# Attention and SwiGLU on one core: a gap inside two weight arrays, and the identity matrix from GpSimd's count

## The chip, the cores and the metric

The kernel runs on one core of a Trainium2 chip. The metric is the device time of one execution in microseconds (us), the median of several runs. Five engines work side by side, each through its own queue in order: TensorE (PE in the profile; PEld are its weight loads), VectorE (DVE), ScalarE (ACT), GpSimd (POOL) and SyncE (SP), which here issues DMAs. They wait for each other by semaphores.

## The reference

Block-causal attention over 8 batches, 8 heads, 576 positions and a head size of 64, and behind it a gated feed-forward (SwiGLU) over all 4608 tokens, all in fp32:

```python
scores = scale * np.matmul(q, k.transpose(0, 1, 3, 2))
scores = np.where(mask, scores, -1000000000.0)      # mask: block of the query >= block of the key, blocks of 64
attn = np.exp(scores - np.max(scores, axis=-1, keepdims=True))
attn = attn / (np.sum(attn, axis=-1, keepdims=True) + 1e-09)
x = np.matmul(attn, v)                              # then [batch, seq, heads * 64]: 4608 tokens x 512
g = x @ w_gate                                      # 512 x 1536
out = (g * (1.0 / (1.0 + np.exp(-g))) * (x @ w_val)) @ w_out
```

q and k are drawn about four times larger than v. The weights arrive as 64-bit floats, which the kernel reads as pairs of 32-bit words and turns into fp32 itself.

## The kernel before

**Products in three.** TensorE multiplies in a rounded fp32 format. Each fp32 matrix is therefore held as a high part and a low remainder, and each product is taken as three: high by high, high by low, low by high (L1100 to L1102 for the products with w_gate and w_val, L1191 to L1193 for those with w_out). In the names a final 0 is the high part and 1 the low one: xhl0_0 and xhl0_1, g_even0 and g_even1.

**Tiles.** The feed-forward goes over 18 tiles of 256 tokens. For each it takes the 1536 columns of w_gate and w_val in twelve chunks of 128, two chunks a step, so six steps a tile and 108 in all. A step is 12 products with the even gate chunk, 12 with the odd one and 24 with w_val's two chunks (4 chunks of the contraction of 512, by 3 products, each 128 x 256 columns), and 12 products with w_out (128 x 512). The weights are the stationary operand of the first 48, x is the moving one; for w_out the hidden values (hhl) are stationary.

**Where the weights lie.** w_gate and w_val stay in SBUF: `g_odd` and `g_even` hold the odd and the even chunks of w_gate, `v_all` all of w_val, each as a high and a low array of [128, 4, columns]. They are allocated in this order: ident, ones and two single columns, g_odd, v_all, a gap of 64 bytes, g_even, and then the pools (v, ob, parts, xhl, wo, hhl, t and so on). Their lengths are such that g_odd and v_all start 64 bytes past a multiple of 128, and g_even and everything behind it at a multiple of 128. `w_at` gives one chunk of 128 columns. Six chunks of w_out are parked, until they are stored, in places of w_gate and w_val that are not yet filled (`AWAY`); the others pass through the pool wo.

**The start.** TensorE turns q and k by products with `ident`, the 128 x 128 identity. VectorE makes it: it fills a row of `t` with 0, 1, 2, ... by doubling (L308 to L311), transposes 32 of them to get each partition's own number (L312), adds 32, 64 and 96 for the other quarters (L315), and compares (L316). GpSimd meanwhile fills v, ob and part of parts with zeros (L260, L281, L234). GpSimd's later work is the maximum over partitions (`partition_all_reduce`, L709).

**The order of the work.** The kernel writes down some thousands of tasks with an engine, an estimated cost and a rank, and `in_order` plays them through once at build time: it takes for each free engine the ready task of lowest rank, and what comes out is the program, with each engine's queue in that order. The change alters neither costs nor ranks nor the number of tasks. What stands before the tasks (the constants, the identity, the first zeros) is issued first.

Of the kernel before, what the change touches and what calls it, by code (L numbers as in the profile page):

```python
# [18 lines left out]
def kernel(  # L19
# [21 lines left out]
    P = 128  # L41
# [156 lines left out]
    g_odd = [const.tile(half_w, F32R, name=f"g_odd{x}") for x in range(2)]  # L198
    v_all = [const.tile(whole_w, F32R, name=f"v_all{x}") for x in range(2)]
    const.tile([P, 16], F32, name="gap")  # L200
    g_even = [const.tile(half_w, F32R, name=f"g_even{x}") for x in range(2)]

    def w_at(which, x, i):

        if which:
            return v_all[x][:, :, i * P : (i + 1) * P]
        return (g_odd if i % 2 else g_even)[x][:, :, i // 2 * P : (i // 2 + 1) * P]

# [86 lines left out]
    pool_of(psum, "gv", 2, [([P, 2 * XT], F32)])  # L297
    pool_of(psum, "po", 1, [([P, 2, DM], F32)])

    first_of = [("v", ""), ("ob", "signs" if wide else "out"), ("parts", "pair"), ("xhl", ""), ("wo", "raw"), ("hhl", "")]  # L300
    for tag, variant in first_of:
        for place in range(len(slots[tag])):
            tiles_of(tag, place, variant)


    scratch = tiles_of("t", 0)[0]
    count, mine = scratch[:, 0:P], scratch[:, P : P + 32]
    nc.vector.memset(count[:, 0:1], 0.0)  # L308
    for i in range(7):
        n = 2**i  # L310
        nc.vector.tensor_scalar(count[:, n : 2 * n], count[:, 0:n], float(n), None, ALU.add)  # L311
    nc.vector.transpose(mine, count[:, 0:32])  # L312
    for i in range(1, P // 32):
        rows = slice(32 * i, 32 * (i + 1))
        nc.vector.tensor_scalar(mine[rows, 0:1], mine[rows, 0:1], 32.0 * i, None, ALU.add)  # L315
    nc.vector.tensor_scalar(ident, count, mine[:, 0:1], None, ALU.is_equal)  # L316

    x_d = dram.tile([DM, NT], F32, name="x_d")
    s_d = dram.tile([H, NT], F32, name="s_d")
# [594 lines left out]
    def weight(i, kind):  # L914
# [11 lines left out]
        wo = Buf("wo", "out") if kind == 2 and not away else None  # L926
        fs = slice(i * P, (i + 1) * P)

        parts = 1 if wo else NDC

        def part(j):
            if wo:
                return wo[0][:, j : j + 1]
            which, c = away or (kind, i)
            return w_at(which, j, c)

# [11 lines left out]

        def words_of(j):
            w = raw[0].rearrange("p (n t) -> p n t", t=1 + wide)[:, :, j]  # L950
            return w.rearrange("p (n m) -> p n m", n=parts)

        y = Buf("ob", "signs") if wide else None


        def signs():
            w = words_of(1).bitcast(F32)
            to = y[0].rearrange("p (n m) t -> p n m t", n=parts)[:, :, :, 1]
            nc.scalar.mul(to, w, 2.0**-60)  # L959

        def scaled():
# [2 lines left out]


        def fraction():
            s = y[0].rearrange("p m t -> p (m t)").bitcast(I32).rearrange("p (n m) -> p n m", n=parts)
            nc.vector.scalar_tensor_tensor(
                words_of(0), words_of(0), 29, s, ALU.logical_shift_right, ALU.bitwise_or
            )  # L970
# [21 lines left out]
        if kind == 2:  # L992
            w_kept[i] = t, wo, part

            def store():
                if wo:
                    nc.sync.dma_start(out=wo_d[i], in_=wo[0].bitcast(F32))
                    return
                for j in range(2):
                    nc.sync.dma_start(  # L1000
                        out=wo_d[i][:, j].rearrange("p (n m) -> p n m", n=parts), in_=part(j).bitcast(F32)
                    )

            t = dma(R, 5e5, store, [t], [wo] if wo else [], 2 if away else 1, packet=512 if away else 4096)
            if away:
                before_place.append((t, away))
# [59 lines left out]
    def feed_forward(j, t0, w, xs):  # L1066
# [19 lines left out]
        def up(i, which, prev):  # L1086
# [3 lines left out]
            for y in range(2):  # L1090

                for ds in [range(NDC)] if j >= FINE else [[d] for d in range(NDC)]:

                    def products(ds=ds, y=y):
                        hi, lo = (w_at(which, k, i + y) for k in range(2))
                        o = ps[0][:, y * w : (y + 1) * w]
                        for d in ds:
                            xhi, xlo = (xs[d][1][k] for k in range(2))
                            first, last = d == 0, d == NDC - 1
                            nc.tensor.matmul(o, lhsT=hi[:, d], rhs=xhi[:, 0:w], start=first, stop=False)  # L1100
                            nc.tensor.matmul(o, lhsT=hi[:, d], rhs=xlo[:, 0:w], start=False, stop=False)  # L1101
                            nc.tensor.matmul(o, lhsT=lo[:, d], rhs=xhi[:, 0:w], start=False, stop=last)  # L1102

                    ts = add(
                        "PE",
                        mm_us(w, w, w) * len(ds),
                        rank(i),
                        products,
                        [ts, *(xs[d][0] for d in ds), w_done[i + y, which]],
                        [ps, *(xs[d][1] for d in ds)],  # L1110
                    )
                    ts.prev = prev
                    prev = ts if j >= FINE else None
# [3 lines left out]
        for i in range(0, NFC, 2):  # L1117
# [41 lines left out]
            for y in range(2):  # L1159
# [3 lines left out]
                else:  # L1163
# [5 lines left out]
                    chain["wo"] = wl  # L1169

                    def w_part(k, wo=wo):
                        return wo[0][:, k : k + 1]

                took.append((wl, wo, w_part, away))

# [7 lines left out]
            for piece in pieces:  # L1183

                def products(i=i, piece=piece, hh=hh, took=took):
                    for y, m in piece:
                        whi, wlo = (took[y][2](k) for k in range(2))
                        bs = slice(y * w + m * P, y * w + (m + 1) * P)
                        po = sums(m).rearrange("p (n m) -> p n m", n=whi.shape[1])
                        hi, lo = hh[0][:, bs], hh[1][:, bs]  # L1190
                        nc.tensor.matmul(po, lhsT=hi, rhs=whi, start=i + y == 0, stop=False)  # L1191
                        nc.tensor.matmul(po, lhsT=hi, rhs=wlo, start=False, stop=False)  # L1192
# [221 lines left out]
```

## Time and profile before

| | |
|---|---|
| median of 3 runs | 1178.03 us (1176.53 to 1178.63) |
| the profiled execution, own time | 1175.4 us |
| its span, first to last instruction | 1173.6 us |
| TensorE busy | 1145.5 us (98%), 8512 matmuls |
| TensorE weight loads | 1024.7 us (87%) |
| VectorE, ScalarE busy | 758.9 us (65%), 620.4 us (53%) |
| GpSimd busy | 325.5 us (28%) |
| mean granted TensorE clock | 0.996 of full speed |
| DMA | 197.40 MB, 168 GB/s mean |

The profile is of one execution and has its own time; comparisons with other kernels go by the medians of runs. A matmul's duration in it is from its start to the modelled end of its pipeline, longer than the distance between two starts: how fast TensorE goes is read from the distances. A share of busy time is a mean over stages; here the first 75 us differ from the rest.

### The profile page before, as it was taken

The numbers are of one execution on the slowest core, as the hardware profiler recorded it, in microseconds if no ns is written. First come the engines' busy times: TensorE is split into PE (matmuls) and PEld (weight loads), VectorE is DVE, ScalarE is ACT, GpSimd is POOL, SyncE is SP. The second block draws the span as 40 slices with busy tenths as digits, with TensorE's granted clock in tenths as the row PEclk, the third lists the DMA queues.
The fourth block names the chain that finished last, engine by engine and source line by source line (L and its number), as shares of the span: only waits on it lengthen the run. The fifth ranks groups of instructions, "written<-read, shape, count | busy, mean of one in ns | idle before, by whom it ended". The sixth has DMA issues, their size and how long they took to land.

```text
span 1173.6 us, 21780 instructions
## 1 busy us (share of the span) xinstructions
PE 1145.5 (98%) x8512; PEld 1024.7 (87%) x8512; DVE 758.9 (65%) x1230; ACT 620.4 (53%) x1114; POOL 325.5 (28%) x139
## 2 busy tenths in 40 slices
PE   5889999999999999999999999999999999999998
PEld 4568778898898989988998899898989899999997
DVE  6988988575887668768575859575767533323222
ACT  6978876546573837465656555555646312212111
POOL 3222100144535251434444334252432500000000
PEclk9989999999999999999999999999999999999999
DMA  8658756766564756656565565655663445444432
GB/s 225 188 151 219 201 187 226 206 178 166 169 148 137 198 164 167 195 166 168 152 188 160 152 177 163 187 146 161 164 202 108 145 148 197 140 167 136 143 134 100
DMA packets 266982, 197.40 MB, mean 168 GB/s; under 512 B 195264, under 2 KB 231376, under 8 KB 266880
## 3 DMA queue, kind: packets, MB, share of 16 engines
q1 hardware_dynamic: 264304, 195.29, 56.9%
q8 instruction: 67, 1.10, 0.4%
q10 hardware_dynamic: 2576, 0.72, 0.3%
q14 instruction: 35, 0.29, 0.1%
HBM read 171.57 MB, written 24.38 MB: 167 GB/s over the span
## 4 chain that ended last, share of the span: by engine, by line
PE 85%; DVE 5%; ACT 4%; DMA 3%; issue 1%; POOL 1%; SPq 1%; ACTq 0%; DVEq 0%; POOLq 0%
PE gv L1100 16%; PE gv L1102 15%; PE gv L1101 15%; PE po L1191 7%; PE po L1193 7%; PE po L1192 7%; PE at L777 7%; PE at L564 6%; DVE sc L733 1%; DVE mx L705 1%; DMA wo<-in_moe_w_val_dram 1%; POOL mx L709 1%; DMA wo<-in_moe_w_out_dram 1%; ACT ob L959 1%; PE at L648 1%
## 5 line engine op out<-in xcount | busy, mean ns | idle before, releaser
L709 POOL PARTITION_ALL_REDUCE mx<-mx x80 | 144.1, 1850 | 408.7 <-issue 135.2
L1100 PE MATMUL gv<-xhl,v_all 128*128 128x256 f32 x864 | 241.8, 280 | 0.8 <-DVE t L1136 0.7
L1102 PE MATMUL gv<-xhl,v_all 128*128 128x256 f32 x864 | 239.7, 277 | 0.0
L1101 PE MATMUL gv<-xhl,v_all 128*128 128x256 f32 x864 | 239.3, 277 | 0.0
L828 POOL PARTITION_ALL_REDUCE mx<-mx x48 | 178.9, 3775 | 201.4 <-DVE mx L705 192.8
L1136 DVE SCALAR_TENSOR_TENSOR t<-t,gv 128x512 f32<-128x512 f32 x108 | 74.0, 685 | 215.4 <-ACT t L1133 215.2
L1100 PEld LDWEIGHTS gv<-xhl,v_all 128*128 128x128 f32 x864 | 162.1, 188 | 4.9 <-issue 2.5
L1101 PEld LDWEIGHTS gv<-xhl,v_all 128*128 128x128 f32 x864 | 162.3, 188 | 0.6
L1102 PEld LDWEIGHTS gv<-xhl,v_all 128*128 128x128 f32 x864 | 162.2, 188 | 0.2
L1133 ACT ACTIVATE t<-gv 128x512 f32<-128x512 f32 x108 | 64.6, 598 | 171.2 <-PE gv L1102 171.1
L1191 PE MATMUL po<-wo,hhl 128*128 128x512 f32 x372 | 147.7, 397 | 0.0
L1192 PE MATMUL po<-wo,hhl 128*128 128x512 f32 x372 | 145.6, 391 | 0.0
L1193 PE MATMUL po<-wo,hhl 128*128 128x512 f32 x372 | 145.1, 390 | 0.2 <-DVE hhl L1149 0.2
L1146 ACT CAST hhl<-t 128x512 fp32r<-128x512 f32 x108 | 67.0, 620 | 132.1 <-DVE t L1141 129.7
L733 DVE TENSOR_TENSOR sc<-sc,mx 128x640 f32<-128x640 f32 (+6 forms) x168 | 122.7, 765 | 11.7 <-POOL mx L709 11.6
L737 ACT ACTIVATE sc<-sc 128x1024 f32<-128x1024 f32 (+3 forms) x104 | 106.0, 1029 | 45.3 <-DVE sc L733 44.9
L1100 PE MATMUL gv<-xhl,g_even 128*128 128x256 f32 x432 | 123.7, 286 | 0.0
L1102 PE MATMUL gv<-xhl,g_even 128*128 128x256 f32 x432 | 122.2, 283 | 0.4 <-DVE g_even L981 0.4
L1101 PE MATMUL gv<-xhl,g_even 128*128 128x256 f32 x432 | 122.1, 283 | 0.0
L1100 PE MATMUL gv<-xhl,g_odd 128*128 128x256 f32 x432 | 120.7, 279 | 0.0
L1101 PE MATMUL gv<-xhl,g_odd 128*128 128x256 f32 x432 | 119.6, 277 | 0.0
L1102 PE MATMUL gv<-xhl,g_odd 128*128 128x256 f32 x432 | 119.6, 277 | 0.0
(171 smaller groups left out, 2368.8 us busy)
## 6 DMA issues: line engine op xcount, KB each, us to landing
wo<-wo_d SPq DMA_DIRECT2D x200, 512.0 KB
out_dram<-ob SPq DMA_DIRECT2D x35, 256.0 KB
v<-in_v_dram SPq DMA_DIRECT2D x64, 128.0 KB
xt<-x_d SPq DMA_DIRECT2D x64, 128.0 KB
rt<-r_d SPq DMA_DIRECT2D x128, 64.0 KB
qk<-in_q_dram SPq DMA_DIRECT2D x112, 72.0 KB
qk<-in_k_dram SPq DMA_DIRECT2D x104, 72.0 KB
x_d<-xu SPq DMA_DIRECT2D x24, 288.0 KB
```

The costliest lines, as they stand in the source:

```text
L709: nc.gpsimd.partition_all_reduce(m, m, channels=P, reduce_op=bass_isa.ReduceOp.max)
L733: nc.vector.tensor_tensor(piece(c), scores_of(c), m, ALU.subtract)
L737: nc.scalar.activation(x, x, AF.Exp)
L777: nc.tensor.matmul(ps[0][own(x), 1 - i if sums else i, q0 - s0 : s1 - s0], lhsT=ones if sums else vt[0][:, 2 * lane + c, own(x)], rhs=sc[0 ...
L828: nc.gpsimd.partition_all_reduce(m, m, channels=P, reduce_op=bass_isa.ReduceOp.add)
L1100: nc.tensor.matmul(o, lhsT=hi[:, d], rhs=xhi[:, 0:w], start=first, stop=False)
L1101: nc.tensor.matmul(o, lhsT=hi[:, d], rhs=xlo[:, 0:w], start=False, stop=False)
L1102: nc.tensor.matmul(o, lhsT=lo[:, d], rhs=xhi[:, 0:w], start=False, stop=last)
L1136: nc.vector.scalar_tensor_tensor(t[0][:, 0:n], t[0][:, 0:n], 1.0, pg[0][:, 0:n], ALU.add, ALU.mult)
L1191: nc.tensor.matmul(po, lhsT=hi, rhs=whi, start=i + y == 0, stop=False)
L1192: nc.tensor.matmul(po, lhsT=hi, rhs=wlo, start=False, stop=False)
L1193: nc.tensor.matmul(po, lhsT=lo, rhs=whi, start=False, stop=i + y == NFC - 1)
```

## The change

Each g_even array becomes two halves of two contraction chunks each, with 16 words (64 bytes) between them; the 64-byte gap ahead of the arrays stays. All views of a chunk get one more dimension (half, chunk, column), for every array, so that one expression serves all; the products take `hi[:, d // 2, d % 2]` in place of `hi[:, d]`. Chunks of w_out that are parked in g_even are stored half by half.

The identity is made by GpSimd's `iota`, which writes column minus partition into `t`, and one VectorE comparison with zero. Its place is now ahead of the first zeros. With that `t` is allocated before v, and with the longer g_even arrays (12416 bytes for 12288) v, ob, parts, xhl, wo and hhl move by 2304 bytes and the pools behind them by 256.

```diff
+    rows_w = NDC * DFF // 4
+    g_even = [const.tile([P, 2, rows_w + 16], F32R, name=f"g_even{x}") for x in range(2)]
...
+        if w is None:
+            w = g_even[x][:, :, 0:rows_w].rearrange("p h (n f) -> p h n f", n=NDC // 2)
+        else:
+            w = w.rearrange("p (h n) f -> p h n f", h=2)
+        return w[:, :, :, i // 2 * P : (i // 2 + 1) * P]
...
+    scratch = tiles_of("t", 0)[0].bitcast(I32)[:, 0:P]
+    nc.gpsimd.iota(scratch, [[1, P]], channel_multiplier=-1)
+    nc.vector.tensor_scalar(ident, scratch, 0, None, ALU.is_equal)
...
-    scratch = tiles_of("t", 0)[0]
-    count, mine = scratch[:, 0:P], scratch[:, P : P + 32]
-    nc.vector.memset(count[:, 0:1], 0.0)
-    for i in range(7):
-        n = 2**i
-        nc.vector.tensor_scalar(count[:, n : 2 * n], count[:, 0:n], float(n), None, ALU.add)
-    nc.vector.transpose(mine, count[:, 0:32])
-    for i in range(1, P // 32):
-        rows = slice(32 * i, 32 * (i + 1))
-        nc.vector.tensor_scalar(mine[rows, 0:1], mine[rows, 0:1], 32.0 * i, None, ALU.add)
-    nc.vector.tensor_scalar(ident, count, mine[:, 0:1], None, ALU.is_equal)
...
+                halves = [slice(0, 2)] if away[0] or away[1] % 2 else [slice(x, x + 1) for x in range(2)]
                 for j in range(2):
-                    nc.sync.dma_start(
-                        out=wo_d[i][:, j].rearrange("p (n m) -> p n m", n=parts), in_=part(j).bitcast(F32)
-                    )
+                    for x in halves:
+                        nc.sync.dma_start(
+                            out=wo_d[i][:, j].rearrange("p (h n m) -> p h n m", h=2, n=parts[1])[:, x],
+                            in_=part(j)[:, x].bitcast(F32),
+                        )
...
-                            nc.tensor.matmul(o, lhsT=hi[:, d], rhs=xhi[:, 0:w], start=first, stop=False)
+                            nc.tensor.matmul(o, lhsT=hi[:, d // 2, d % 2], rhs=xhi[:, 0:w], start=first, stop=False)
```

GpSimd's queue at the start of the program, before. A row "ISA" without operands ahead of other work loads a code library of GpSimd; here it is library 1, which has the reduction over partitions (the rows "ISA" with mx).

```order
L260 MEMSET v_0_78 128x640
L260 MEMSET v_0_80 128x640
L281 MEMSET ob_0_82 128x512
L281 MEMSET ob_0_84 128x512
L234 MEMSET parts_1_87 128x64
L234 MEMSET parts_1_90 128x64
L709 ISA
L709 ISA mx_0_181<-mx_0_181 128x256 [waits DVE_49]
```

The same place after:

```order
L311 ISA
L311 IOTA t_0_78 128x128
L269 MEMSET v_0_81 128x640
L269 MEMSET v_0_83 128x640
L290 MEMSET ob_0_85 128x512
L290 MEMSET ob_0_87 128x512
L243 MEMSET parts_1_90 128x64
L243 MEMSET parts_1_93 128x64
L710 ISA
L710 ISA mx_0_170<-mx_0_170 128x256 [waits DVE_49]
```

Ahead of the zeros stand two new rows, a library load (L311; it is library 0, which has the count) and the count. The load ahead of the reductions is there in both.

VectorE's queue at the start, before, from its last constant to the first maximum:

```order
L192 MEMSET seen 128x1
L308 MEMSET t_0_117 128x1
L311 TENSOR_SCALAR t_0_117<-t_0_117 128x1
L311 TENSOR_SCALAR t_0_117<-t_0_117 128x2
L311 TENSOR_SCALAR t_0_117<-t_0_117 128x4
L311 TENSOR_SCALAR t_0_117<-t_0_117 128x8
L311 TENSOR_SCALAR t_0_117<-t_0_117 128x16
L311 TENSOR_SCALAR t_0_117<-t_0_117 128x32
L312 STREAM_TRANSPOSE t_0_117<-t_0_117 128x32
L311 TENSOR_SCALAR t_0_117<-t_0_117 128x64
L315 TENSOR_SCALAR t_0_117<-t_0_117 32x1 x3
L316 TENSOR_SCALAR ident<-t_0_117 128x128
```

And after:

```order
L190 MEMSET unseen 64x1
L192 MEMSET seen 128x1
L312 TENSOR_SCALAR ident<-t_0_78 128x128
L703 COPY mx_0_170<-at_0_160 128x2x128
L706 TENSOR_TENSOR mx_0_170<-mx_0_170,at_0_160 128x2x128
```

Twelve instructions are gone; the comparison is left, and now waits for GpSimd. On TensorE, ScalarE and the rest of VectorE and GpSimd the order is the same, and SyncE has four more stores.

## Rows read from the trace of the kernel before

**Rows 1.** Busy time by stretch (instructions); clock, DMA share and GB/s at the end.

```profile
0.00:75.00 75.00, 54.29 (x417) 37.74 (x418) 59.43 (x132) 56.79 (x112) 22.44 (x26) 0.95 0.72 189
75.00:1150.00 1075.00, 1071.39 (x7965) 969.07 (x7964) 694.87 (x1092) 560.24 (x998) 303.03 (x113) 1.00 0.57 169
```

**Rows 2.** TensorE's waits after 75 us: who for whom, us, times, longest.

```profile
PE at L777 <- ACT sc L469: 2.0, 2, 1.1
...
PE at L1191 <- DMA wo<-wo_d: 0.2, 1, 0.2
```

**Rows 3.** Timeline of TensorE in one late step: start us, duration, line, operands.

```profile
1109.11 0.28 PE L1100 MATMUL gv<-xhl,g_even 128*128 128x256 f32 x1
1109.22 0.28 PE L1101 MATMUL gv<-xhl,g_even 128*128 128x256 f32 x1
1109.34 0.28 PE L1102 MATMUL gv<-xhl,g_even 128*128 128x256 f32 x1
...
1110.54 0.28 PE L1100 MATMUL gv<-xhl,g_odd 128*128 128x256 f32 x1
...
1111.90 0.28 PE L1100 MATMUL gv<-xhl,v_all 128*128 128x256 f32 x1
```

**Rows 4.** TensorE's busy time with g_even alone, by stretch (number of products).

```profile
200.00:400.00 200.00, 30.23 (x216) 1.00 0.63 175
400.00:1173.60 773.60, 126.17 (x948) 1.00 0.53 158
```

**Rows 5.** The same with g_odd alone.

```profile
400.00:1173.60 773.60, 121.06 (x948) 1.00 0.53 158
```

**Rows 6.** Timeline of all engines at the start; in brackets the idle time before.

```profile
0.73 1.20 POOL L260 MEMSET v<- 128x640 f32 x2 [0.29 <-POOLq L1397]
...
1.69 0.97 SPq L754 DMA_DIRECT2D v<-in_v_dram  x2
...
2.85 0.23 POOL L234 MEMSET parts<- 128x64 f32 x2
2.98 3.77 SPq L387 DMA_DIRECT2D qk<-in_q_dram  x6
...
4.44 1.22 PE L411 MATMUL gv<-ident,qk 96*128 96x96 f32 x6 [4.44 <-DVE ident L316]
...
8.74 0.42 DVE L702 COPY mx<-at 128x256 f32<-128x256 f32 x1 [4.36 <-ACT mx L482]
...
8.78 2.44 PE L411 MATMUL gv<-ident,qk 96*128 96x96 f32 x12 [0.97 <-DMA qk<-in_q_dram]
9.09 0.41 DVE L705 TENSOR_TENSOR mx<-mx,at 128x256 f32<-128x256 f32 x1
...
9.59 2.11 POOL L709 PARTITION_ALL_REDUCE mx<-mx  x2 [6.51 <-DVE mx L705]
...
11.73 1.02 DVE L733 TENSOR_TENSOR sc<-at,mx 128x512 f32<-128x512 f32 x2 [2.24 <-POOL mx L709]
...
12.67 0.68 DVE L968 SCALAR_TENSOR_TENSOR wo<-wo,ob 128x512 int32<-128x512 int32 x1
...
13.90 0.69 DVE L973 SCALAR_TENSOR_TENSOR wo<-wo 128x512 int32<-128x512 int32 x1 [0.55 <-ACT wo L963]
...
15.75 4.20 POOL L709 PARTITION_ALL_REDUCE mx<-mx  x4 [4.05 <-DVE mx L705]
```

**Rows 7.** GpSimd's instructions of line 709 up to 12 us: count, duration ns, first and last start.

```profile
L709 POOLq MODIFY_POOL_CONFIG  x2: 7/7/7, 3.1 to 3.1; - x2
```

**Rows 8.** Waits of SyncE's queue in the first 30 us.

```profile
SPq L387 <- DMA qk<-in_k_dram: 0.8, 1, 0.8
```

**Rows 9.** The chain that ended last, 50 to 76 us: start, us, what.

```profile
55.77 4.29 PE po L777 x40
...
67.03 7.20 PE at L777 x40
```

## The prediction before the run

> **What bounds the kernel now.** I read the busy times by stretch first. From 75 us to 1150 us TensorE is busy 1071.39 of 1075.00 us; in the first 75 us only 54.29 us [rows 1]. So the program has two parts with different limits: a start-up in which TensorE waits for others, and a long part in which it alone sets the time. In the long part it waits for a DMA once, for 0.2 us, and five times in all for 3.4 us, the longest 2.0 us [rows 2]. A nanosecond off a matmul there comes off the time, and a microsecond lost at the start is not won back, as there are only 3.4 us of idle time to lose it in.
>
> Then the matmuls in order of time. In a step of the feed-forward the twelve products with an even gate chunk start at 1109.11, 1109.22, 1109.34 and so on; the first with the odd chunk starts at 1110.54 and the first with v_all at 1111.90 [rows 3]. Twelve even ones take 1.43 us, twelve odd ones 1.36 us, though shape, buffers of x and instructions are the same. The first even spacing is 0.11 us like those of the odd ones, the eleven others 0.12. The same difference over the whole stretch: from 400 us on 948 products with g_even hold TensorE 126.17 us and as many with g_odd 121.06 us [rows 4, 5].
>
> What differs is where the arrays lie. By the kernel's sizes g_odd and v_all start 64 bytes past a multiple of 128, g_even and all that is allocated after it, x's halves (xhl) among them, at multiples of 128. So with g_even the weights that are loaded for the next product and the columns that stream for this one have equal addresses modulo 128; with g_odd and v_all they are 64 apart.
>
> Last the start, in order of time. GpSimd's memset of v starts at 0.73; SyncE's queue puts the first loads of v at 1.69 and behind them six loads of q from 2.98 on; TensorE starts at 4.44, released by `ident`, and again at 8.78, released by a load of q; GpSimd's first reduction starts at 9.59 and the next four at 15.75, each released by VectorE's maximum [rows 6]. Between the last memset and the first reduction lie 6.51 us of idle time, and in their first moment, at 3.1 us, two records called MODIFY_POOL_CONFIG [rows 6, 7]: they belong to the row without operands that stands before the reductions in GpSimd's order, which loads the code library (number 1) that has the reduction.
>
> **The change part by part.** *The gap.* With 64 bytes between the two halves of each g_even array, the contraction chunks 0 and 1 stay at equal places, and 2 and 3 become like g_odd's: six products of twelve. Of the eleven long spacings six go, of 0.07/11 = 0.0064 us each, so 0.04 us a step. From 200 us on there are (216 + 948)/12 = 97 steps [rows 4]: 3.8 us. Before 200 us I count nothing: TensorE's spacings there are mixed, and up to 75 us it is not the limit. Bounds: nothing (if the place is not the cause), and 97 x 0.074 = 7.2 us if all eleven go because the new distances (x now lies 256 bytes on, modulo 512, against g_odd, v_all and half of g_even) matter beyond 128 bytes. I take 3.8, since odd and even rows differ in nothing else that I find.
>
> The Trainium skill speaks against this edit: "SBUF — State Buffer", "Who interferes with whom", gives TensorE two independent read ports, one for the moving operand and one for the weights, and says that TensorE never waits on anyone. By that rule the gap gives 0 and not 3.8 us; the 0.07 us between two groups of equal products [rows 3] disagree with it, but show no cause by themselves.
>
> *The identity.* Twelve small VectorE instructions go. That gives nothing: VectorE idles 4.36 us until 8.74 right behind them [rows 6]. In their place GpSimd counts, and the order has one more row without operands ahead of the count: a load of library 0. After the memsets library 1 has to be loaded again, as before. The length of a load stands nowhere in the trace. From below it is nothing (library 0 might be there already). From above the nearest row is the idle time of 6.51 us, into which the load of library 1 fits without delaying the reduction: that starts 0.09 us after its releaser, as the next one does. I take 6.2 us for either load, near that row, since the reduction is the only row by which a load shows at all; the first one may well be longer, because nothing bounds it.
>
> The Trainium skill ("GPSIMD Engine Reference", "2.1 Instruction dispatch") has about 6 us, 5.95 measured, for the first call to a freshly loaded kernel, without an instruction in the profile. By it the start would lose 5.5 us, and the sum would be +1.7; no run here shows it yet.
>
> What waits for that load? Everything on GpSimd's queue behind it, which before started at 0.73: the count (about 0.3 us, between a 64-column memset, two in 0.23, and a 640-column one, two in 1.20 [rows 6]), the memsets of v, and so the third entry of SyncE's queue, the load of v, which waits for them. So SyncE stands still for 6.2 + 0.3 = 6.5 us with all later inputs behind it: the rest of q, and the first weights. One thing is won back: SyncE's wait of 0.8 us for loads of k [rows 8], which ScalarE's queue issues and which will long be there. The transposes that began at 8.78, released by a load of q, come 6.5 - 0.8 = 5.7 us later. `ident` itself is ready at about 0.73 + 6.2 + 0.3 + 0.4 = 7.6, so TensorE starts at 7.7 and not 4.44: 3.3 late, hidden by the 5.7.
>
> The second load starts when the memsets end: 0.73 + 6.2 + 0.3 + 2.35 = 9.6 (before: from 0.73 to 3.08 [rows 6]). The first reduction then starts at 15.8, not 9.59, and ends 2.1 later, at 17.9. Behind it VectorE has 1.02 + 0.68 + 0.69 + 0.42 + 0.41 = 3.2 us of queue [rows 6] up to the maximum of the next reductions: 21.2 against 15.75, 5.5 late. That is just inside the 5.7. From there every wait of TensorE up to 75 us is ended by ScalarE or VectorE, which are as late, so the 5.7 us go through to the end.
>
> *The rest at nothing.* Four more stores are issued (the two even parked pieces, each half in two): 4 x 0.49 us on SyncE's queue [rows 6], covered as TensorE waits 0.2 us for a DMA after 75 us; at most 2.0 without that cover. Casts into g_even write the same elements through one more dimension. All other addresses move by multiples of 256 bytes, so they keep their place modulo 128.
>
> **The sum** against the profiled execution, 1175.4 us (span 1173.6 and 1.8 around it): +5.7 - 3.8 = +1.9 us. That run lies 2.6 us under the median of the runs shown, 1178.03. On the median: 1179.9 us.
>
> **The rivals.** *The loads are longer, and the second decides* (slower). Price of the second path: its lateness is T0 + T1 - 6.9 us (5.5 at 6.2 each), of the first T0 - 0.5; the second is the later one from T1 = 6.4 on. With 8 us each the start loses 9.1 us: +9.1 - 3.8 = +5.3, 1183.3 us. For it: the first load has no bound, and the second now runs beside weight loads that ran later before. Against it: the load of before fitted into 6.51 us beside loads of its own.
>
> *The library is at hand, or its load costs next to nothing* (faster). Then the start stays where it is, as GpSimd's memsets and count end before 4 us: -3.8, 1174.2 us. For it: the two records take 7 ns each [rows 7]. Against it: the program ends with library 1 in place, and runs again and again.
>
> *The place is not the cause*, by the skill's rule on the ports: the even products would be slow as the first of a step. Then 1178.03 + 5.7 = 1183.7 us. Against it: the first even spacing is a short one and the eleven behind are equal.
>
> *The distances matter beyond 128 bytes* and all long spacings go: 5.7 - 7.2 = -1.5, 1176.5 us.
>
> One thing can move any of these: near 67 us TensorE's granted clock lies at the lower of its two levels, 1.2 GHz (0.95 over the first 75 us [rows 1]; forty products take 7.20 us there and 4.29 us ten us earlier [rows 9]). With a later start that may fall elsewhere or not at all, up to 2.9 us to the better, and as much to the worse if it comes twice.
>
> **How the numbers follow.** A measurement of this kernel tells a difference from 0.2%, 2.4 us. My case, 0.44: mostly within 2.4 us, 1177.5 to 1182. Longer loads 0.23, place not the cause 0.10: slower. Load for nothing 0.15: faster. Larger distances 0.08: about no change. So faster 0.18, same 0.41, slower 0.41. The range of 8 in 10 goes from the case without a load, 1174.2, to loads of 8 us with a little more, 1185.5.
>
> **What would show it.** The first transpose near 7.7 us, the second near 14.5, the first reduction near 15.8 with an idle stretch before it that no engine ends, the count near 7 us; in late steps twelve even products in 1.39 us and odd and v_all ones unchanged at 1.36 and 2.72. Wrong: a count near 1 us (no load), twelve even products in 1.43 or 1.36, or a v_all spacing that has changed.

## The result and the profile after

The changed kernel takes 1181.31 us (median of 20 runs, 1179.26 to 1185.14), the kernel before 1176.84 (20 runs, 1174.90 to 1179.15). The ratio is 1.0037 with an interval of 1.0029 to 1.0045: 4.4 us slower, 3.4 to 5.3. Forecast were 1.9 us slower and a range of 1174.2 to 1185.5. That holds the result, and slower was one of the two likeliest outcomes; the likeliest case's own size was too small.

The profiled execution has a time of 1185.14 us and a span of 1183.4, the slowest of its 20. So the spans of the two profiles, 9.8 us apart, are not the effect of the change. A part of it is TensorE's clock in the first 75 us: its mean is 0.89 of full speed and not 0.95 [rows 1].

```profile
0.00:75.00 75.00, 51.23 (x363) 36.09 (x363) 50.89 (x106) 51.81 (x99) 20.15 (x25) 0.89 0.65 169
75.00:1150.00 1075.00, 1069.26 (x7951) 964.04 (x7952) 701.68 (x1102) 564.39 (x1007) 304.23 (x115) 1.00 0.58 169
```

The chain of waits shows the clock by three groups of forty equal products (start, us, what). One takes 4.29 us as before, at 2.4 GHz; two take 6.55 and 6.01, partly at 1.2 GHz, where the kernel before had one slow group [rows 9]. In this execution the granted clock is at 1.2 GHz in three stretches, 23.1 to 33.3, 50.4 to 57.2 and 77.7 to 81.1 us; in the profile before it is so from 66.1 to 72.9 and in the last 2 us.

```profile
52.64 6.55 PE po L778 x40
...
66.02 4.29 PE po L778 x40
...
77.28 6.01 PE at L778 x40
```

The start, in order of time, all engines (answers to [rows 6]):

```profile
7.96 0.23 POOL L311 IOTA t<- 128x128 int32 x1 [7.52 <-issue]
8.16 1.19 POOL L269 MEMSET v<- 128x640 f32 x2
8.23 2.31 DVE L312 TENSOR_SCALAR ident<-t 128x128 f32<-128x128 int32 x1 [7.09 <-POOL t L311]
8.80 0.91 SPq L755 DMA_DIRECT2D v<-in_v_dram  x2
9.76 3.00 SPq L388 DMA_DIRECT2D qk<-in_q_dram  x6
10.23 0.23 POOL L243 MEMSET parts<- 128x64 f32 x2
10.60 1.22 PE L412 MATMUL gv<-ident,qk 96*128 96x96 f32 x6 [10.60 <-DVE ident L312]
14.60 2.44 PE L412 MATMUL gv<-ident,qk 96*128 96x96 f32 x12 [0.64 <-DMA qk<-in_q_dram]
15.24 0.41 DVE L706 TENSOR_TENSOR mx<-mx,at 128x256 f32<-128x256 f32 x1
16.62 2.15 POOL L710 PARTITION_ALL_REDUCE mx<-mx  x2 [6.16 <-DVE mx L706]
21.98 2.11 POOL L710 PARTITION_ALL_REDUCE mx<-mx  x2 [3.21 <-DVE mx L706]
```

The count starts at 7.96 us, behind idle time that no engine ends ("issue"): that is the first code load. Its records are at 0.8 us, those of the second at 10.7 (count, duration in ns, first and last start; [rows 7] had one pair, at 3.1):

```profile
L311 POOLq MODIFY_POOL_CONFIG  x2: 11/11/11, 0.8 to 0.8; - x2
...
L710 POOLq MODIFY_POOL_CONFIG  x2: 7/7/7, 10.7 to 10.7; - x2
```

From 0.8 to 7.96 is 7.1 us, from 10.7 to the first reduction at 16.62 is 5.9. That reduction's maximum was ready at 15.65 (15.24 + 0.41); before, a reduction started 0.09 us behind its maximum [rows 6], now 0.97. So the second load shows too. SyncE's queue waits 7.1 us for the zeros of v (in the waits of that queue; [rows 8] had 0.8 for k, and that is gone):

```profile
SPq L755 <- POOL v L269: 7.1, 1, 7.1
```

In a late step the even group takes 1.40 us from its first start to that of the odd one (1.43 in [rows 3]) and the odd one 1.37 (1.36 but for rounding); a value group takes 2.72 as before:

```profile
1110.76 0.28 PE L1105 MATMUL gv<-xhl,g_even 128*128 128x256 f32 x1
...
1112.16 0.28 PE L1105 MATMUL gv<-xhl,g_odd 128*128 128x256 f32 x1
...
1113.53 0.28 PE L1105 MATMUL gv<-xhl,v_all 128*128 128x256 f32 x1
```

Over the whole stretch from 400 us on (time, number of products; first line g_even, second g_odd, two views), a product with g_even holds TensorE for 131.0 ns, where it was 133.1 [rows 4]; one with g_odd for 127.9, where it was 127.7 [rows 5].

```profile
400.00:1183.40 783.40, 125.74 (x960) 124.24 (x960) 0.00 (x0) 0.00 (x0) 1.00 0.54 160
...
400.00:1183.40 783.40, 122.75 (x960) 115.35 (x960) 0.00 (x0) 0.00 (x0) 1.00 0.54 160
```

So the even group did get shorter, by 2.1 ns x 12 = 25 ns a step, and not by the 39 that the sum's 3.8 us come to in 97 steps.

### The profile page after: what moved, and what is told of

Its sections match the earlier page's. It is cut to its first block, busy times and chain, and to the rows that moved or that the text cites. A ratio compares the mean times of both kernels' runs of the same rounds, so it can differ in the third digit from the quotient of the medians.

```text
span 1183.4 us, 21775 instructions
## 1 busy us (share of the span) xinstructions
PE 1150.0 (97%) x8512; PEld 1027.0 (87%) x8512; DVE 760.0 (64%) x1218; ACT 621.4 (53%) x1114; POOL 324.4 (27%) x140
## 4 chain that ended last, share of the span: by engine, by line
PE 84%; ACT 5%; DMA 4%; DVE 4%; issue 2%; SPq 1%; POOL 0%; DVEq 0%; POOLq 0%; ACTq 0%
PE gv L1105 15%; PE gv L1106 15%; PE gv L1107 15%; PE po L1196 7%; PE po L1198 7%; PE po L1197 7%; PE at L778 7%; PE at L565 5%; ACT sc L738 1%; ACT sc L456 1%; PE po L778 1%; DVE mx L706 1%; DMA wo<-in_moe_w_out_dram 1%; PE at L438 1%; ACT ob L960 1%
```

## The experiments

Differences in us are the ratio times the median of the kernel before in the same comparison, with its interval.

### The two halves of the change, each alone

**The gap alone**: the changed kernel, with its addresses, and the twelve VectorE instructions for the identity.

```diff
-    scratch = tiles_of("t", 0)[0].bitcast(I32)[:, 0:P]
-    nc.gpsimd.iota(scratch, [[1, P]], channel_multiplier=-1)
-    nc.vector.tensor_scalar(ident, scratch, 0, None, ALU.is_equal)
+    scratch = tiles_of("t", 0)[0]
...
+    count, mine = scratch[:, 0:P], scratch[:, P : P + 32]
+    nc.vector.memset(count[:, 0:1], 0.0)
...
+    nc.vector.tensor_scalar(ident, count, mine[:, 0:1], None, ALU.is_equal)
```

> The gap as in the changed kernel, the identity as before (twelve small VectorE instructions, no count on GpSimd), every array at the changed kernel's address. Theory (equal places modulo 128 cost about 6.4 ns per long spacing, six of eleven go): 3.8 us faster than before, about 1173, and in the trace twelve even products of a late step in 1.39 us. If place is not the cause: 0. If distances beyond 128 bytes matter: 7.2 us faster and twelve in 1.36 us. The start must look as before (reduction near 9.6 us).

Measured: 1175.14 us, ratio 0.9985 (0.9976 to 0.9994): 1.8 us faster, 0.7 to 2.8. About half of the 3.8. One reason is in the late steps, where twelve even products take 1.41 us and not 1.39:

```profile
1108.45 0.28 PE L1114 MATMUL gv<-xhl,g_even 128*128 128x256 f32 x1
...
1109.86 0.28 PE L1114 MATMUL gv<-xhl,g_odd 128*128 128x256 f32 x1
```

A second is in the early ones. TensorE's timeline near 300 us shows the start of an odd group and of the value group behind it, first in the run with the gap alone:

```profile
299.36 0.28 PE L1114 MATMUL gv<-xhl,g_odd 128*128 128x256 f32 x1
...
300.77 0.28 PE L1114 MATMUL gv<-xhl,v_all 128*128 128x256 f32 x1
```

and at the same step of the kernel before:

```profile
298.67 0.28 PE L1100 MATMUL gv<-xhl,g_odd 128*128 128x256 f32 x1
...
300.03 0.28 PE L1100 MATMUL gv<-xhl,v_all 128*128 128x256 f32 x1
```

The odd group, whose place modulo 128 is as before, takes 1.41 us with the gap and 1.36 without.

**The count alone**: the kernel before with the identity as changed, g_even without a gap inside.

```diff
+    scratch = tiles_of("t", 0)[0].bitcast(I32)[:, 0:P]
+    nc.gpsimd.iota(scratch, [[1, P]], channel_multiplier=-1)
+    nc.vector.tensor_scalar(ident, scratch, 0, None, ALU.is_equal)
...
-    scratch = tiles_of("t", 0)[0]
-    count, mine = scratch[:, 0:P], scratch[:, P : P + 32]
...
-    nc.vector.tensor_scalar(ident, count, mine[:, 0:1], None, ALU.is_equal)
```

> The count on GpSimd as in the changed kernel, g_even without a gap. Theory of the prediction (SyncE's queue stands for the first code load, the rest of q comes late): 5.7 us slower than before, about 1182.5. Rival, from the trace of the changed kernel (first load 7.1 us, compare on VectorE 2.3 us instead of 0.3, first reduction 7.0 us later than before): the second load decides, 6 to 8 us slower, 1183 to 1185. Second rival: lower clock at the start adds up to 6 us more than that in a run with three low stretches.

Measured: 1183.76 us, ratio 1.0055 (1.0042 to 1.0068): 6.5 us slower, 4.9 to 8.0. Its profile has the mean clock of the kernel before (0.996) and a span 7.5 us longer. The timeline of its start has the count at 8.36 and the first reduction 7.4 us later than in [rows 6]:

```profile
8.36 0.23 POOL L301 IOTA t<- 128x128 int32 x1 [7.92 <-issue]
...
17.03 2.15 POOL L700 PARTITION_ALL_REDUCE mx<-mx  x2 [6.18 <-DVE mx L696]
```

The two halves add up: 6.5 - 1.8 = 4.7, against 4.4 measured for both. The q transposes come at 15.27, 6.5 us later than before, so the start does not yet say which path decides.

### Which path makes the start longer

**Two loads, nothing else late**: identity by VectorE, zeros first, and a count on GpSimd that nobody reads, so that the reductions need a second load.

```diff
     nc.vector.tensor_scalar(ident, count, mine[:, 0:1], None, ALU.is_equal)
+    spare = const.tile([P, 64], I32, name="spare")
+    nc.gpsimd.iota(spare, [[1, 64]], channel_multiplier=-1)
```

> The kernel before, identity by VectorE, and a count of 64 columns on GpSimd behind its memsets whose result nobody reads: so GpSimd loads two code libraries, but SyncE's loads of v do not wait for one and the identity is as early as before. Only the reductions come late (first at about 16.5 instead of 9.6 us). If SyncE's wait alone made the start longer (the prediction): the reductions still are 6.8 us late here, so by the prediction's second path 5 to 7 us slower, 1183. If slack between the reductions and TensorE covers the lateness once q and v come in time: 0 to 3 us slower. TensorE's transposes must start at 4.44 and 8.78 as before.

Measured: 1183.50 us, ratio 1.0060 (1.0044 to 1.0077): 7.1 us slower, 5.2 to 9.1. Its timeline of the start:

```profile
4.44 1.22 PE L413 MATMUL gv<-ident,qk 96*128 96x96 f32 x6 [4.44 <-DVE ident L316]
...
8.56 2.43 PE L413 MATMUL gv<-ident,qk 96*128 96x96 f32 x12 [0.63 <-DMA qk<-in_q_dram]
...
10.48 0.18 POOL L318 IOTA spare<- 128x64 int32 x1 [7.40 <-issue]
...
16.76 2.15 POOL L711 PARTITION_ALL_REDUCE mx<-mx  x2 [6.10 <-issue]
```

TensorE gets identity and q as early as before, SyncE's queue does not stand, and still the time is lost: the first reduction starts at 16.76 us, released by nothing but the load, 7.2 us late [rows 6], and the next four start at 22.11, 6.4 late. This path alone is enough for the whole price, as far as the interval tells.

**A select in place of the count**, meant to be in the reductions' library; g_even has no gap inside.

```diff
+    scratch = tiles_of("t", 0)[0][:, 0:P]
+    nc.gpsimd.memset(scratch, 1.0)
+    nc.gpsimd.affine_select(out=ident, in_=scratch, pattern=[[1, P]], base=0, channel_multiplier=-1, compare_op=ALU.is_equal, fill=0.0)
...
-    nc.vector.tensor_scalar(ident, count, mine[:, 0:1], None, ALU.is_equal)
```

> The identity by GpSimd from ones with a select that lies in the same code library as the reductions: one load and not two, and the program's order puts the memsets of v ahead of it. g_even without a gap. SyncE does not wait, the reductions do not wait for a second load; only the identity is late (about 10.7 us instead of 4.4, TensorE's first transposes with it). If a late identity is hidden by the second transposes (before: 8.78), as the prediction had it: 0 to 3 us slower than before. If it is a path of its own to the first maximum and reduction: 5 to 6.5 us slower, with the first reduction near 15.5 us, its releaser VectorE.

Measured: 1182.86 us, ratio 1.0061 (1.0044 to 1.0078): 7.2 us slower, 5.2 to 9.2. A miss in its setting: the select and the reduction behind it each have an idle stretch of a load ahead of them in the timeline, so it loads twice like the count.

```profile
10.84 0.28 POOL L302 TENSOR_SCALAR_AFFINE_SELECT ident<-t 128x128 f32<-128x128 f32 x1 [7.77 <-issue]
...
17.34 2.15 POOL L700 PARTITION_ALL_REDUCE mx<-mx  x2 [6.02 <-issue]
```

It repeats the result, reduction 7.75 us late, 7.2 us slower, but does not separate the paths, as the identity is late here too. Whether a single load, or SyncE's wait alone, would cost as much was not tried.

### What the places of weights and x do

**All apart**: the 64 bytes stand behind g_even and not ahead of it. g_odd, v_all and x keep their addresses.

```diff
-    const.tile([P, 16], F32, name="gap")
     g_even = [const.tile(half_w, F32R, name=f"g_even{x}") for x in range(2)]
+    const.tile([P, 16], F32, name="gap")
```

> The kernel before with the 64 bytes behind g_even instead of ahead of it: g_odd, v_all and g_even all lie 64 bytes past a multiple of 128, x's halves at multiples, so no product of gate or value has equal places. Everything else has its address of before. Theory (place is the cause): all eleven long spacings of an even step go, 97 steps x 0.07 us = 7 us faster than before, about 1170, twelve even products in 1.36 us like the odd ones. If even products are slow as the first of a step: 0 and still 1.43 us.

Measured: 1185.71 us, ratio 1.0072 (1.0060 to 1.0085): 8.5 us slower, 7.1 to 10.0, where 7 us faster was expected. The late step in TensorE's timeline:

```profile
1107.82 0.40 PE L1191 MATMUL po<-wo,hhl 128*128 128x512 f32 x1
...
1110.55 0.28 PE L1100 MATMUL gv<-xhl,g_even 128*128 128x256 f32 x1
...
1111.97 0.28 PE L1100 MATMUL gv<-xhl,g_odd 128*128 128x256 f32 x1
...
1113.38 0.28 PE L1100 MATMUL gv<-xhl,v_all 128*128 128x256 f32 x1
...
1116.20 0.40 PE L1191 MATMUL po<-wo,hhl 128*128 128x512 f32 x1
```

Even 1.42, odd 1.41, value 2.82 us. The even group is only a little better than with equal places, and the odd and value groups are worse by 0.05 and 0.10 us, though not one of their addresses has changed. A late step loses 0.15 us and wins 0.02. So the time of a product is not set by its own places alone.

The starts show what it is instead. A row of such products runs at one of three distances: 113.3 ns (1.36 us for twelve, "fast"), 117.7 ("slow") and, with equal places, 120. At unequal places both fast and slow occur, and **a group keeps the distance of the group that it follows**. I counted, over the whole trace of each kernel, the odd groups that follow their even group directly (82 in each): fast, if the twelfth product starts 1.25 us behind the first, slow at 1.30.

| kernel | places of the even group | fast odd groups of 82 |
|---|---|---|
| before | all twelve equal | 81 |
| count alone | all twelve equal | 81 |
| after | first six equal | 71 |
| gap alone | first six equal | 69 |
| all apart | none | 6 |
| low parts equal | every third | 4 |
| equal last | last six equal | 2 |
| wo and hhl moved | none | 3 |
| hhl moved | none | 0 |
| cut at 64, cut at 128 | none | 3, 6 |

With all apart, 80 even groups stand directly behind products with w_out, and all 80 are slow. A value group directly behind an odd one has the odd one's distance in 85 of 85 cases before and in 86 of 86 with all apart (groups of six products or more). Of the 13 slow odd groups with the gap alone, none has its even group directly behind products with w_out; in ten cases that even group stands behind value products.

The group directly ahead is not all, though. Twelve odd groups stand directly behind attention products of 192 columns. Eleven of them are slow in the kernel before and eleven are fast with all apart, at the same addresses of both. So something besides the group directly ahead and these addresses plays a part.

**None apart**: the 64 bytes stand ahead of g_odd, so that every gate and value product has equal places.

```diff
+    const.tile([P, 16], F32, name="gap")
     g_odd = [const.tile(half_w, F32R, name=f"g_odd{x}") for x in range(2)]
     v_all = [const.tile(whole_w, F32R, name=f"v_all{x}") for x in range(2)]
-    const.tile([P, 16], F32, name="gap")
```

> The kernel before with the 64 bytes ahead of g_odd: g_odd, v_all and g_even all lie at multiples of 128, as x's halves do, so all products of gate and value have equal places. Theory (place is the cause, 6 to 7 ns a spacing): the 36 products of a step with g_odd and v_all get as slow as the even ones, 97 x 36 x 6.5 ns = 23 us slower than before, about 1200, and twelve odd products take 1.43 us. If the place is not the cause: 0, and odd products stay at 1.36 us.

Measured: 1196.17 us, ratio 1.0157 (1.0143 to 1.0171): 18.5 us slower, 16.8 to 20.1. The odd group takes 1.44 us, as expected of the place:

```profile
1114.02 0.28 PE L1100 MATMUL gv<-xhl,g_odd 128*128 128x256 f32 x1
...
1115.46 0.28 PE L1100 MATMUL gv<-xhl,v_all 128*128 128x256 f32 x1
```

So the place is a cause: nothing but addresses differs from the kernel before. It is not the whole of it, as the run with all apart shows.

**Low parts equal**: the 64 bytes between g_even0 and g_even1.

```diff
-    const.tile([P, 16], F32, name="gap")
-    g_even = [const.tile(half_w, F32R, name=f"g_even{x}") for x in range(2)]
+    g_even = [const.tile(half_w, F32R, name="g_even0")]
+    const.tile([P, 16], F32, name="gap")
+    g_even.append(const.tile(half_w, F32R, name="g_even1"))
```

> The kernel before with the 64 bytes between g_even0 and g_even1: g_even0 (high parts of the weights) 64 bytes past a multiple of 128, g_even1 (low parts) at a multiple, as x's halves. One product of three has equal places with its own weights. Theory of the prediction (each product pays for its own place): four long spacings of twelve, -4.4 to -5 us, about 1172.5, twelve even products in 1.39 us and odd ones in 1.36. Rival, from the runs so far (back-to-back products keep one of two rhythms, 113.3 or 117.75 ns, until something breaks it; products at equal places, 120 ns, are followed by the fast one): if a third of equal places is enough to break the slow rhythm, the same; if not, odd ones in 1.41 us, value ones in 2.82, and slower than before by 3 to 8 us, as with all apart.

Measured: 1185.75 us, ratio 1.0083 (1.0069 to 1.0097): 9.8 us slower, 8.1 to 11.4. A third of equal places leaves the row slow.

**Equal places last**: the gap alone, and late steps take the even chunk's contraction in the order 2, 3, 0, 1. No address differs from the gap alone, and the work is the same.

```diff
+                        if len(ds) > 1 and not which and (i + y) % 2 == 0:
+                            ds = [2, 3, 0, 1]
                         for d in ds:
-                            first, last = d == 0, d == NDC - 1
+                            first, last = (d == ds[0], d == ds[-1]) if len(ds) > 1 else (d == 0, d == NDC - 1)
```

> The gap alone (chunks 0 and 1 at equal places, 2 and 3 apart, identity by VectorE), and late steps take the even chunk's products in the order of chunks 2, 3, 0, 1, so the equal places come last. If each product pays for its own place: 1.40 us for twelve as with the gap alone, and its time. If the rhythm is carried: six at 117.75 behind the down products and six at 120, 1.42 to 1.43 us, nearly as before, and the odd group always at 1.36, also in the early steps where the gap alone had 1.41 in 13 of 82. About the time of before, within 1.5 us.

Measured: 1184.52 us, ratio 1.0073 (1.0059 to 1.0087): 8.6 us slower, 6.9 to 10.2, where no change was expected.

```profile
1108.88 0.28 PE L1116 MATMUL gv<-xhl,g_even 128*128 128x256 f32 x1
...
1110.30 0.28 PE L1116 MATMUL gv<-xhl,g_odd 128*128 128x256 f32 x1
...
1111.71 0.28 PE L1116 MATMUL gv<-xhl,v_all 128*128 128x256 f32 x1
```

This is the sharpest pair of the study: the same products at the same addresses, only their order within the even group turned, and the odd group behind goes from 1.36 to 1.41 us. Equal places bring the fast distance only if they come first, directly behind the products with w_out. Six equal ones at the end do not; my picture that equal products "break" the slow row wherever they stand was wrong.

**A cut product**: all apart, and in each late step the even group's second product in two pieces of columns (64 and 192; in a second run 128 and 128).

```diff
-                            nc.tensor.matmul(o, lhsT=hi[:, d], rhs=xlo[:, 0:w], start=False, stop=False)
+                            split = first and w == 2 * P and j >= FINE and not which and (i + y) % 2 == 0
+                            cuts = [0, 64, w] if split else [0, w]
+                            for b0, b1 in zip(cuts, cuts[1:]):
+                                nc.tensor.matmul(o[:, b0:b1], lhsT=hi[:, d], rhs=xlo[:, b0:b1], start=False, stop=False)
```

> The kernel with all apart (1.41 us for twelve, slow rhythm behind every down product), and in each late step the second product of the even chunk issued as 64 and 192 columns. Nothing of the places changes. If the rhythm is carried from product to product and a 192-column product leaves it fast (as behind the attention's 192-column products in that run): the even group pays about 0.05 us for the cut, the odd and value groups come back to 1.36 and 2.72 us; against all apart 8 to 11 us faster, against before -2 to -4 us, about 1174. If the places alone made odd and value products slow there: still 1.41 and 2.82 us, and 5 us slower than all apart.

> [...] If any interruption of the row of equal products brings the fast rhythm: odd and value groups at 1.36 and 2.72 us and -3 to -5 us against before. If what matters is where the interrupted product ends, the rhythm may stay slow: 8 to 10 us slower than before.

Measured: 1193.02 us, ratio 1.0140 (1.0121 to 1.0158), and 1192.54, ratio 1.0139 (1.0125 to 1.0152): 16 us slower. Either cut costs the even group 0.1 us more. With the cut at 64 columns the odd group starts at 1111.53 and gives way to the value group at 1112.94, 1.41 us later:

```profile
1111.53 0.28 PE L1100 MATMUL gv<-xhl,g_odd 128*128 128x256 f32 x1
...
1112.94 0.28 PE L1100 MATMUL gv<-xhl,v_all 128*128 128x256 f32 x1
```

An interruption of the row by itself does not bring the fast distance.

**hhl moved**: all apart, and hhl, the weights of the w_out products, 64 bytes past a multiple of 128, so that these products have unequal places too.

```diff
+        if tag == "hhl":
+            const.tile([P, 16], F32, name="gap2")
         for place in range(len(slots[tag])):
             tiles_of(tag, place, variant)
+    const.tile([P, 16], F32, name="gap3")
```

> All three gate and value arrays 64 bytes past a multiple of 128, as in the run with all apart, and hhl (the weights of the down products) too, wo's buffers at multiples of 128: no product of the feed-forward has equal places. If the slow rhythm is begun by the down products with equal places (227 ns steady, 232 to 236 in the first five): 12 even, 12 odd and 24 value products in 1.36, 1.36, 2.72 us, some 7 us faster than before, 1170. If the slow rhythm needs only that nothing breaks it: as with all apart, 1.41 us and 8 us slower than before. If places of hhl and wo cost the down products themselves (213.3 would be 512 columns at 2.4 GHz, 226.7 is measured): up to 12 x 13 ns x 97 = 15 us more off.

Measured: 1191.52 us, ratio 1.0127 (1.0108 to 1.0146): 14.9 us slower, 12.7 to 17.2. Twelve w_out products take 2.80 us in its late step, and 2.73 with all apart (1107.82 to 1110.55), from which nothing but the place of hhl differs:

```profile
1113.99 0.40 PE L1194 MATMUL po<-wo,hhl 128*128 128x512 f32 x1
...
1116.79 0.28 PE L1103 MATMUL gv<-xhl,g_even 128*128 128x256 f32 x1
```

The trace has their distances alternating between 231 and 236 ns, where at equal places they settle at 227. With wo and hhl in their old places twelve take 2.73 to 2.77 us in the late steps of the other runs, so 2.80 is outside what the rows ahead do to them. For these products of 512 columns unequal places are the dearer ones: that equal places cost and unequal ones are free does not hold for both shapes.

**wo and hhl moved**: all apart, and the same gap ahead of wo's buffers, so that wo, hhl and all gate and value weights have the same place and only x another.

```diff
+        if tag == "wo":
+            const.tile([P, 16], F32, name="gap2")
         for place in range(len(slots[tag])):
             tiles_of(tag, place, variant)
+    const.tile([P, 16], F32, name="gap3")
```

> The kernel with all apart (g_odd, v_all, g_even 64 bytes past a multiple of 128, x's halves at multiples), and wo's buffers and hhl 64 bytes past a multiple too. Down products stay equal among themselves; the first weights of an even chunk now lie at a place equal to that of wo's columns, which stream as they are loaded, and still apart from x's. If the first load behind a down product sets the rhythm by its place against wo's columns: the fast rhythm from the first product on, twelve even, odd and value products in 1.36 us, 6 to 7 us faster than before, 1170. If its place against x's columns sets it (or nothing but equal products behind the down ones breaks the slow rhythm): as with all apart, 1.41 us and 8 us slower than before.

Measured: 1187.67 us, ratio 1.0098 (1.0081 to 1.0115): 11.5 us slower, 9.5 to 13.5. The odd group stays slow:

```profile
1113.73 0.28 PE L1103 MATMUL gv<-xhl,g_odd 128*128 128x256 f32 x1
...
1115.15 0.28 PE L1103 MATMUL gv<-xhl,v_all 128*128 128x256 f32 x1
```

So first weights at the place of wo's columns, which stream ahead of them, do not bring the fast distance behind w_out; first weights at the place of x did, in the four kernels at the head of the table.

## Why the prediction was right, and where it was not

**The mechanisms.** Both halves went the way that the sum gave them: the identity slower, the gap faster, the first larger than the second. Both terms came out on the same side: +6.5 measured for 5.7, -1.8 for 3.8. Together that is 2.8 us, about the distance from the +1.9 forecast to the +4.4 measured. Clear of the noise is only the gap's: 5.7 lies inside the 4.9 to 8.0 of the count alone, 3.8 outside the 0.7 to 2.8 of the gap alone.

**The identity's term** was put down to SyncE's queue: 5.7 us by late q, with the reductions 5.5 late "just inside". That step failed. The q transposes do come 5.8 us late (14.60 for 8.78), but the first reduction comes 7.0 late, and the run with two loads and nothing else late shows that the reductions are enough for the whole price. This is the mechanism of the rival in which the second load decides, at less than its 8 us a load. The sum did not lead to it: by the rows the first load takes 7.1 us and the second 5.9, and with these the prediction's own formulas give 6.1 us by the reductions and 6.6 by SyncE's queue. The first is what came, the next four reductions starting at 21.98 for 15.75, 6.2 late. The second is not: the load of v is 7.1 us late, and up to the q transposes the queue won back 1.3 us and not 0.8. That 5.7 lies near 6.5 is partly luck, then: two paths of nearly the same length, and the sum took the other one.

The first transposes were forecast at 7.7 us and came at 10.60. The load is 0.9 longer, and the comparison takes 2.31 us and not 0.4: it starts at 8.23 and ends at 10.54, as GpSimd's last zeros end (10.23 + 0.23 for two). Before, the comparison was fp32 and ran after the zeros. The Trainium skill ("SBUF — State Buffer", "Who interferes with whom") has VectorE and GpSimd share a pair of ports as an exclusive lock; the trace agrees with it, in that the comparison ends with the zeros. The integer input is not needed for such a wait, as the kernel before shows: there six fp32 instructions of 1 to 32 columns, most of them beside the zeros, take 2.16 us, and one of 64 columns behind them 0.19.

```profile
1.20 2.16 DVE L311 TENSOR_SCALAR t<-t 128x1 f32<-128x1 f32 x6
...
3.39 0.19 DVE L311 TENSOR_SCALAR t<-t 128x64 f32<-128x64 f32 x1
```

Those of 2, 4 and 8 columns take 0.57, 0.45 and 0.45 us and each end 0.02 to 0.03 us behind one of the zero writes. The long comparison cost nothing by itself: the reduction waited 0.97 us longer for its load.

The Trainium skill's figure for a first call ("GPSIMD Engine Reference", "2.1 Instruction dispatch": about 6 us, 5.95 measured) fits the load of the reductions' library: 5.9 us here, and 5.8 to 6.0 in the three other runs with two loads, from the MODIFY_POOL_CONFIG rows to the reduction. The load ahead of it, for the count or the select, is longer in all four: 7.1 to 7.8 us from the same rows. That it is the program's first is not shown to be the reason: in the kernel before, the first load is that of the reductions, and its rows at 3.1 and the reduction at 9.59 leave it 6.5 us at most (or nothing, if the execution ahead had left that library in place).

**The gap's term** was six spacings of 6.4 ns in 97 steps. The late even group saved 25 ns a step and not 39: in the kernel after, its eleven spacings are 113, 124, 121, 117, 118, 118, 117, 120, 119, 113 and 113 ns, so of the long ones only the last two have become short. And a second effect was missing from the sum: in the gap-alone run 13 of 82 odd groups run slow for 1 before, all but one of them before 360 us, as the row behind a shortened even group can stay at 117.7 ns. Added up over the two traces, from each product to the next where these are at most 125 ns apart, the even products win 2.3 us, the odd ones lose 0.6 and the value ones 0.8. That leaves 0.8 us, and 1.8 (0.7 to 2.8) were measured.

What failed there is a premise of the change part: that odd and even rows differ "in nothing else" than their own places, so that a product's spacing belongs to that product. The even rows were slow, and were what made the 36 products behind them fast. By that premise all apart would have been the best layout, 7 us faster; it is 8.5 slower.

**The Trainium skill's rule on two independent ports** ("SBUF — State Buffer", "Who interferes with whom"), weighed against the gap, would have given 0 for it and no effect of any address. With none apart, 18.5 us come from addresses alone; the measurement decides against the rule here.

**The clock** moved as the closing remark allowed, to the worse: three stretches at 1.2 GHz in the profiled execution. That may be a part of why it is the slowest of the 20 (mean clock 0.991), but another at 0.990 took 1182.61 us. The difference of the medians does not rest on it, as the count alone shows: 6.5 us slower, with the clock of before in its profile.

**The rest at nothing** held: TensorE waits for a DMA of parked weights once, 0.3 us, behind 75 us. One row was misread, without effect on the sum: the 2.0 us of [rows 2] are two waits together, the longest 1.1, and the 3.4 us are six waits and not five.

**Still open**: why a row at unequal places has two distances, and why the slow one follows the products with w_out unless x and the first weights lie at equal places. The runs show when, not how, and what sets the distance behind the attention products is not known either. Only one offset, 64 bytes, was tried, so that 128 is the modulus is not shown. Which of the two paths would decide if there were only one load is open too.

## What to carry to other kernels

A slow group in a row of back-to-back matmuls may be what keeps the group behind it fast: before speeding it up, time the groups behind it in a version where it is fast, and move addresses only with the whole row in view. A GpSimd instruction from another code library than the work behind it costs two loads in a row, some 7 and 6 us here, and the first reductions pay for both even if everything else is on time. The best version of this study is the gap alone, 0.15% faster than before (0.06 to 0.24%) and by the two ratios some 6 us faster than the changed kernel.

## What was not expected of the hardware

- Products of 128 x 256 columns at 2.4 GHz follow each other at 113.3, 117.7 or 120 ns, and the first two are handed on from group to group at unchanged addresses: 81 of 82 odd groups are fast in the kernel before and 6 of 82 with all apart, 69 of 82 with the gap alone and 2 of 82 with the same addresses in another order.
- The sign of the effect turns with the shape: 64 bytes apart, twelve products of 512 columns take 2.80 us and not 2.73.
- Two code loads in a row are not alike: the one for the count or the select takes 7.1 to 7.8 us, the one for the reductions behind it 5.8 to 6.0.
- A VectorE comparison of 128 x 128 beside GpSimd's zeros took 2.31 us; the fp32 one behind them takes 0.28.
